# A fused set-attention and maxout kernel: x cast straight into SBUF, transposed on TensorE, four token groups to a score tile, eight PSUM banks in one pool

## The chip, the core and the metric

The kernel runs on one core of one Trainium2 chip. A core has five engines with an instruction queue each: TensorE (PE in the profile, with its weight loads listed apart as PEld), VectorE (DVE), ScalarE (ACT), GpSimd (POOL) and SyncE (SP). Matmul results land in PSUM, which has eight banks of 128 partitions x 512 f32; DVE and ACT move them to SBUF ("eviction"). The metric is the device time of one execution in microseconds (us).

## What is computed

There are B = 4 batches of N = 12544 tokens with C = 128 features, m = 32 inducing points, and a maxout layer with d_ff = 1024.

```python
def mab(q, kv):
    s = scale * (q @ kv.transpose(0, 2, 1))
    s = s - s.max(-1, keepdims=True)
    a = np.exp(s)
    a /= a.sum(-1, keepdims=True) + 1e-09
    return a @ kv
h = mab(I, x)                # (B, 32, C): 32 inducing points look at all tokens
y = mab(x, h)                # (B, N, C): each token looks at the 32 rows of h
g = np.maximum(y @ w1, y @ w2)
out = g @ w_out
```

Both kernels use max(y w1, y w2) = y w1 + relu(y (w2 - w1)), and since y is a weighted mean of the rows of h, both push h through the weights first: hwd = h (w2 - w1) and m1 = h w1 w_out are small. Per token there remain the 32 exponentials E2, relu(E2 hwd) with 1024 values, its product with w_out, E2 m1, and a division by the sum of E2. The maxima are not subtracted.

## The kernel before

**Phase 1** (for each batch, tokens in blocks of 2048, that is 16 groups of 128): GpSimd's queue casts x from f32 to f16, DRAM to DRAM, into `xf16` (`emit_cast`, line 70). SyncE's queue then loads it twice: transposed by a DMA transpose into `xT` (line 113) and plain into `xnat` (line 117). TensorE makes the scores (line 129, 16 matmuls of 32 columns), ACT the exponential `ETg` (line 137), and TensorE accumulates h and its divisor in one PSUM bank over the whole batch (line 152, 16 matmuls of 129 columns a block). `emit_smalls` turns that into hT4, hwdrep (hwd, once for each quarter of the partitions) and m1aug4.

**Phase 2** (tokens in blocks of 512, a "tick"): one matmul gives the scores of 512 tokens with the 32 rows of h repeated four times over the 128 partitions (`emit_s2T`, line 227), and one exponential on ACT evicts them (line 231), so that all four quarters hold the same E2T. `emit_dT_group` (lines 251 to 264) uses the quarters as four row tiles of TensorE: four matmuls of 32 rows for four of the eight 128-wide slices of d_ff. Each fills a bank (tags dT0 to dT3), and the eight results of a tick are evicted with relu, the even ones by DVE (line 264), the odd ones by ACT (line 260). `emit_final_pair_mm` (lines 285 and 293) adds up nine matmuls for each of two token groups; DVE divides (lines 311 and 312), and GpSimd's queue stores 512 tokens at a time (line 323).

PSUM is shared out by tag: four banks for dT, two for the final pairs, one ("psA") for all score tiles, one ("haug") for the accumulation and the small steps. Phase 1 of batch b+1 is spread over the ticks of batch b by `tick_jobs`; the emission order and the pools set the order on each engine.

Of the kernel before, what the change touches and what calls it, by code (L numbers as in the profile page):

```python
# [12 lines left out]
ALU = mybir.AluOpType  # L13

T_BLK = 2048
T_BLK2 = 512
RELU_ON_ACT = (1, 3, 5, 7)
# [3 lines left out]
def kernel(  # L21
# [9 lines left out]
    nc = tc.nc  # L31

# [4 lines left out]
    assert C == 128 and M == 32 and J % 128 == 0  # L37
    scale = 1.0 / math.sqrt(C)

    p1_starts = list(range(0, N, T_BLK))  # L40
    p1_sizes = [min(T_BLK, N - s) for s in p1_starts]
    p2_starts = list(range(0, N, T_BLK2))
    p2_sizes = [min(T_BLK2, N - s) for s in p2_starts]
    NB1 = len(p1_starts)
    NB2 = len(p2_starts)
    for s in p1_sizes + p2_sizes:
        assert s % 128 == 0
    MAXCH1 = T_BLK // 128
    MAXCH2 = T_BLK2 // 128

    consts = ctx.enter_context(tc.tile_pool(name="consts", bufs=1))
    xtp = ctx.enter_context(tc.tile_pool(name="xtp", bufs=1))
    xnp = ctx.enter_context(tc.tile_pool(name="xnp", bufs=1))
    sb2 = ctx.enter_context(tc.tile_pool(name="sb2", bufs=2))
    sb3 = ctx.enter_context(tc.tile_pool(name="sb3", bufs=3))
    relup = ctx.enter_context(tc.tile_pool(name="relup", bufs=3))
    outp = ctx.enter_context(tc.tile_pool(name="outp", bufs=3))
    psum = ctx.enter_context(tc.tile_pool(name="psum", bufs=1, space=bass.MemoryType.PSUM))
    dramp = ctx.enter_context(tc.tile_pool(name="dramp", bufs=1, space=bass.MemoryType.DRAM))

    def psum_tile(name, shape, tag, bufs):
        return psum.tile(shape, F32, name=name, tag=tag, bufs=bufs)

    identity32 = consts.tile([M, M], F32, name="identity32")
    make_identity(nc, identity32)

    xf16 = [dramp.tile([N, C], F16, name=f"xf16_{b}", tag=f"xf16_{b}") for b in range(B)]

    def emit_cast(b, r0, r1):
        nc.gpsimd.dma_start(out=xf16[b][r0:r1], in_=x[b, r0:r1])  # L70

    b0_rows = [0, T_BLK, 2 * T_BLK, 4 * T_BLK, N]
    for i in range(len(b0_rows) - 1):
        emit_cast(0, b0_rows[i], b0_rows[i + 1])

    ind_sb = consts.tile([M, C], F32, name="ind_sb")
    nc.sync.dma_start(ind_sb, inducing)
    indT_ps = psum_tile("indT_ps", [C, M], "psA", 1)
    nc.tensor.transpose(indT_ps, ind_sb, identity32)
    inducingT = consts.tile([C, M], F16, name="inducingT")  # L80
    nc.vector.tensor_copy(out=inducingT, in_=indT_ps)

    w1f = consts.tile([C, NJB, 128], F16, name="w1f")
    nc.gpsimd.dma_start(out=w1f, in_=moe_w1.rearrange("c (jb j) -> c jb j", j=128))
    w2f = consts.tile([C, NJB, 128], F16, name="w2f")
    nc.gpsimd.dma_start(out=w2f, in_=moe_w2.rearrange("c (jb j) -> c jb j", j=128))
    w21f = consts.tile([C, NJB, 128], F16, name="w21f")
    nc.vector.tensor_sub(w21f, w2f, w1f)  # L88
    woutp = consts.tile([128, NJB, C], F16, name="woutp")
    nc.gpsimd.dma_start(  # L90
        out=woutp, in_=moe_w_out.rearrange("(jb j) c -> j jb c", j=128)
    )

    xT_tiles = [xtp.tile([C, N], F16, name=f"xT{i}", tag=f"xT{i}") for i in range(2)]
    NXNAT = 3
    xnat_tiles = [
        xnp.tile([128, MAXCH1, 132], F16, name=f"xnat{i}", tag=f"xnat{i}")
        for i in range(NXNAT)
    ]
    for t in xnat_tiles:  # L100
        nc.gpsimd.memset(t[:, :, 128:129], 1.0)

    st = [dict() for _ in range(B)]
    xnat_ctr = [0]

    def emit_p1_dma(b, ib):
        n0 = p1_starts[ib]
        tb = p1_sizes[ib]
        nch = tb // 128
        xT = xT_tiles[b % 2]  # L110
        if ib == 0:
            st[b]["haug"] = psum_tile(f"haug_b{b}", [128, 132], "haug", 1)
# [306 lines left out]
```

## Time and profile before

| | |
|---|---|
| median of 3 runs | 493.05 us (492.4 to 495.18) |
| span of the profiled execution, first to last instruction | 490.7 us |
| TensorE busy / its weight loads | 396.0 / 281.7 us |
| DVE busy / ACT busy | 349.8 / 279.1 us |
| relu evictions on DVE, 128x512 | 384, 683 ns each |
| relu evictions on ACT, 128x512 | 384, 599 ns each |
| score exponentials of phase 2 on ACT, 128x512 | 96, 600 ns each |
| mean granted TensorE clock | 0.997 |

The profile reports one execution. Its time beside the span is not recorded; the median of the runs is 2.35 us above the span. Busy times of TensorE overlap (a matmul's record runs from its start to its modelled end), so distances between starts say more than the sum. In a timeline row stand start, duration, engine, line, operation, output<-inputs and count; in brackets the engine's idle time before it and what ended it.

### The profile page before, as it was taken

What the parts mean: (1) busy time and instruction counts of PE and PEld (TensorE: products, weight loads), DVE (VectorE), ACT (ScalarE), POOL (GpSimd) and SP (SyncE); (2) the same over time, 40 slices, a digit from 0 to 9 for tenths busy, and PEclk for the clock granted to TensorE, in tenths of its full rate; (3) what the DMA queues carried; (4) which work ended last, traced back from release to release, by engine and by line L of the source; (5) the groups of instructions that cost most, each with busy time, mean ns of one, the idle gap of its engine ahead of it and who ended that gap; (6) DMA issues with size and microseconds to landing.
All of it is one profiled execution on the core that took longest, in us unless ns stands there. A gap on an engine that the chain in (4) does not pass through costs nothing.

```text
span 490.7 us, 12616 instructions
## 1 busy us (share of the span) xinstructions
PE 396.0 (81%) x5289; PEld 281.7 (57%) x5289; DVE 349.8 (71%) x818; ACT 279.1 (57%) x533; POOL 86.2 (18%) x132
## 2 busy tenths in 40 slices
PE   0000005589999999899999998999999989999995
PEld 0000005437777776577777775777777746666664
DVE  0000000059889899889899998989889989999995
ACT  1000001157777776677777666777767667777772
POOL 5110000001112111112111121211122112121212
PEclk9999999999999999999999999999999999999998
DMA  8999999999973468336655561444222212222222
GB/s 172 184 233 208 224 202 229 209 232 216 223 152 97 134 166 156 98 100 162 153 95 153 148 157 55 108 123 117 71 67 66 87 33 87 67 74 78 65 87 76
DMA packets 111769, 65.84 MB, mean 134 GB/s; under 512 B 104640, under 2 KB 104672, under 8 KB 111200
## 3 DMA queue, kind: packets, MB, share of 16 engines
q0 software_dynamic: 9968, 39.33, 30.5%
q1 hardware_dynamic: 101744, 25.71, 27.6%
q8 instruction: 41, 0.67, 0.6%
q14 instruction: 16, 0.13, 0.1%
HBM read 40.12 MB, written 38.54 MB: 160 GB/s over the span
## 4 chain that ended last, share of the span: by engine, by line
issue 75%; POOL 15%; DMA 8%; POOLq 1%
POOL out_dram L323 15%; DMA xf<-in_x_dram 8%; POOLq L323 0%; POOL xf L70 0%; POOLq L414 0%; POOL m1aug_b L218 0%; POOL identity masks.py:199 0%; POOL identity masks.py:197 0%; POOLq masks.py:199 0%; POOLq L218 0%; POOLq L403 0%
## 5 line engine op out<-in xcount | busy, mean ns | idle before, releaser
L264 DVE TENSOR_SCALAR relu_b_n<-dT_b_n_j 128x512 f16<-128x512 f32 (+1 forms) x400 | 257.0, 673 | 28.8 <-PE dT_b_n_j L251 22.3
L260 ACT ACTIVATE relu_b_n<-dT_b_n_j 128x512 f16<-128x512 f32 (+1 forms) x400 | 214.3, 590 | 57.8 <-PE dT_b_n_j L251 57.5
L293 PE MATMUL outp_b_n_p<-woutp,relu_b_n 128*128 128x128 f16 x3136 | 219.2, 219 | 0.0
L293 PEld LDWEIGHTS <-relu_b_n 128*128 128x128 f16 x3136 | 192.4, 98 | 1.1 <-issue 1.1
L323 POOL DMA_DIRECT2D out_dram<-outsb_b_n x100 | 75.0, 750 | 371.1 <-DVE outsb_b_n L312 360.0
L251 PE MATMUL dT_b_n_j<-E2T_b_n,hwdrep_b 32*128 32x512 f16 (+1 forms) x800 | 117.9, 381 | 1.0 <-DVE relu_b_n L264 0.5
L285 PE MATMUL outp_b_n_p<-m1aug_b,E2T_b_n 128*128 128x129 f16 x392 | 88.3, 225 | 0.0
L312 DVE TENSOR_TENSOR outsb_b_n<-outp_b_n_p,rp_b_n_p 128x256 f32<-128x256 f32 x196 | 82.5, 421 | 4.6
L231 ACT ACTIVATE E2T_b_n<-s2T_b_n 128x512 f16<-128x512 f32 (+1 forms) x100 | 59.2, 592 | 42.1 <-PE s2T_b_n L227 40.7
L137 ACT ACTIVATE ET_b_n<-sTg_b_n 128x512 f16<-128x512 f32 (+1 forms) x28 | 15.2, 544 | 102.6 <-PE sTg_b_n L129 102.2
L129 PE MATMUL sTg_b_n<-inducingT,xT 128*128 128x32 f16 x392 | 14.5, 180 | 68.5 <-DMA xT<-xf 68.3
L251 PEld LDWEIGHTS <-hwdrep_b 32*128 32x128 f16 x800 | 33.9, 91 | 57.8 <-issue 39.6
L285 PEld LDWEIGHTS <-E2T_b_n 128*128 128x128 f16 x392 | 37.9, 97 | 44.2 <-issue 40.8
L163 DVE RECIPROCAL hrecip_b<-haug_b 32x1 f32<-32x1 f32 x4 | 0.6, 156 | 76.2 <-PE haug_b L152 76.2
L129 PEld LDWEIGHTS <-xT 128*128 128x128 f16 x392 | 12.7, 98 | 70.0 <-DMA xT<-xf 69.6
L152 PE MATMUL haug_b<-xnat,ET_b_n 128*32 128x129 f16 x392 | 32.3, 243 | 12.7 <-DMA xnat<-xf 12.7
L227 PE MATMUL s2T_b_n<-xT,hT_b 128*128 128x512 f16 (+1 forms) x100 | 38.5, 385 | 0.0
L152 PEld LDWEIGHTS <-ET_b_n 128*32 128x32 f16 x392 | 27.1, 107 | 15.2 <-issue 8.7
L311 DVE RECIPROCAL rp_b_n_p<-outp_b_n_p 128x2 f32<-128x2 f32 x196 | 31.5, 161 | 2.8 <-PE outp_b_n_p L293 2.3
L88 DVE TENSOR_TENSOR w21f<-w2f,w1f 128x1024 f16<-128x1024 f16 x1 | 0.7, 693 | 19.5 <-DMA w2f<-in_moe_w_dram 19.5
L70 POOL DMA_DIRECT2D xf<-in_x_dram x16 | 8.2, 511 | 29.8 <-DMA xf<-in_x_dram 24.8
L227 PEld LDWEIGHTS <-hT_b 128*128 128x128 f16 x100 | 9.9, 99 | 4.5 <-issue 4.5
(29 smaller groups left out, 32.9 us busy)
## 6 DMA issues: line engine op xcount, KB each, us to landing
out_dram<-outsb_b_n POOLq DMA_DIRECT2D x96, 256.0 KB, 2.8
xnat<-xf SPq DMA_DIRECT2D x24, 512.0 KB, 4.8
xf<-in_x_dram POOLq DMA_DIRECT2D x12, 784.0 KB, 28.2
xf<-in_x_dram POOLq DMA_DIRECT2D x1, 1088.0 KB, 16.2
xf<-in_x_dram POOLq DMA_DIRECT2D x2, 512.0 KB, 6.2
xf<-in_x_dram POOLq DMA_DIRECT2D x1, 1024.0 KB, 11.4
out_dram<-outsb_b_n POOLq DMA_DIRECT2D x4, 128.0 KB, 2.2
xT<-xf SPq DMA_TRANSPOSE x28, 5.9
```

Of the source, the lines that this page charges most:

```text
L129: nc.tensor.matmul(out=sTg[:, k * M : (k + 1) * M], lhsT=xT[:, n0 + 128 * k : n0 + 128 * (k + 1)], rhs=inducingT, start=True, stop=True,)
L152: nc.tensor.matmul(out=haug[0:M, 0:129], lhsT=ETg[:, k, :], rhs=xn[:, k, 0:129], start=(gchunk == 0), stop=(last and k == nch - 1),)
L227: nc.tensor.matmul(out=s2T_ps[:, 0:tb], lhsT=hT4, rhs=xT[:, n0 : n0 + tb], start=True, stop=True)
L231: nc.scalar.activation(out=E2T[:, 0:tb], in_=s2T_ps[:, 0:tb], func=AF.Exp, scale=scale)
L251: nc.tensor.matmul(out=dT_ps[:, 0:tb], lhsT=hwdrep[32 * q : 32 * (q + 1), jb // 4, 128 * (jb % 4) : 128 * (jb % 4 + 1)], rhs=E2T[32 * q : ...
L260: nc.scalar.activation(out=relu_sb[:, jb, 0:tb], in_=dT_ps[:, 0:tb], func=AF.Relu)
L264: nc.vector.tensor_scalar(out=relu_sb[:, jb, 0:tb], in0=dT_ps[:, 0:tb], scalar1=0.0, scalar2=None, op0=ALU.max,)
L285: nc.tensor.matmul(out=op_ps[:, kk_i, 0:129], lhsT=E2T[:, tslice], rhs=m1aug4[:, 0:129], start=True, stop=False,)
L293: nc.tensor.matmul(out=op_ps[:, kk_i, 0:128], lhsT=relu_sb[:, jb, tslice], rhs=woutp[:, jb, :], start=False, stop=(jb == NJB - 1),)
L311: nc.vector.reciprocal(out=rp[:, 0:npair, :], in_=op_ps[:, 0:npair, 128:129])
L312: nc.vector.tensor_mul(out_sb[:, 2 * pair : 2 * pair + npair, :], op_ps[:, 0:npair, 0:128], rp[:, 0:npair, :].broadcast_to((128, npair, 128)),
L323: nc.gpsimd.dma_start(out=out[b * N + n0 : b * N + n0 + tb, :].rearrange("(k p) c -> p k c", p=128), in_=out_sb[:, 0:nch, :],)
```

## The change

The kernel is written anew; only the arithmetic stays.

- **Loads.** `load_x` reads 16 groups of f32 from DRAM with a cast into an SBUF tile `xn` (ten tiles). A partition now holds consecutive tokens ("(p k)"), so one partition's piece of a load is 8 KB of f32. The DRAM copy, the DMA transposes and the second load are gone. SyncE's queue loads only the inducing points and the three weight matrices, in f32.
- **Transposes.** `p1_transpose` transposes each group on TensorE against an identity, eight into one bank in f16; DVE evicts one bank of a block, ACT the other.
- **Phase 1.** The accumulation has x as the stationary operand and 32 columns moving, restarts with each block and is added up in SBUF by DVE (`hacc`). The divisor is summed from the exponentials, by GpSimd from batch 1 on (`eacc`), and spread over the partitions by a matmul with ones. m1 comes from one product w1 w_out made once at the start (`w1out`).
- **Phase 2.** Tokens go in blocks of 2048 (n = 16 groups; smaller ones at the ends). `stage` makes the scores of four different sets of 512 tokens with four column tiles of TensorE, one for each quarter of the partitions, and one exponential evicts them. `burst` u makes slice u of d_ff for all four quarters, four row-tiled matmuls into four banks. `final` p handles two groups; since a quarter of E2 now belongs to other tokens, m1 has four variants that are zero outside their quarter. The finals of a block run behind the bursts of the next one, one final for each burst.
- **PSUM and order.** All eight banks are one pool. A list of estimated times (`Model`) picks, while the program is built, the bank that it expects free first, and DVE or ACT for each relu. The order on each engine is the written one (`manual_schedule`).

```diff
-    def emit_cast(b, r0, r1):
-        nc.gpsimd.dma_start(out=xf16[b][r0:r1], in_=x[b, r0:r1])
+    def pick(self, n, ready):
+        return min(
+            ("DVE", "ACT"), key=lambda e: max(self.t[e], ready + self.SEM) + self.cost(e, n)
+        )
...
+    xr = x.rearrange("b (p k) c -> b p k c", p=128)
...
+    def load_x(b, i):
+        k0, n = p1_blocks[i]
+        nc.gpsimd.dma_start(out=xn_of(b, i)[:, 0:n, :], in_=xr[b, :, k0 : k0 + n, :])
...
-        nc.sync.dma_start_transpose(xT[:, n0 : n0 + tb], xf16[b][n0 : n0 + tb, :])
+                for j in range(m):
+                    nc.tensor.transpose(ps[:, j, :], xn[:, g + j, :], identity16)
...
+                eng = "DVE" if (g // 8) % 2 == 0 else "ACT"
...
-                out=haug[0:M, 0:129],
-                lhsT=ETg[:, k, :],
-                rhs=xn[:, k, 0:129],
+                    out=ps[:, 0:M],
+                    lhsT=xn[:, j, :],
+                    rhs=et[:, j, :],
...
+                nc.gpsimd.tensor_add(out=acc, in0=acc, in1=et[:, 0:n, :])
...
+            def stage(self):
+                bi, ps = bank([128, 512])
+                for q in range(4):
+                    c0, t = self.chunks(q)
+                    nc.tensor.matmul(
+                        out=ps[32 * q : 32 * (q + 1), 0 : self.width],
+                        lhsT=st[self.b]["hT4"][:, 32 * q : 32 * (q + 1)],
+                        rhs=xT_tiles[self.b % 2][:, c0 : c0 + t, :],
...
+                        tile_position=(0, 32 * q),
...
+                for jj in range(jpb):
+                    for q in range(4):
+                        bi, ps, qt, j0 = banks[q]
+                        jb = j0 + jj
+                        nc.tensor.matmul(
+                            out=ps[:, jj * w : (jj + 1) * w],
+                            lhsT=st[self.b]["hwd"][32 * q : 32 * (q + 1), 128 * jb : 128 * (jb + 1)],
+                            rhs=self.e2[32 * q : 32 * (q + 1), 0:w],
...
+                for q in range(4):
+                    bi, ps, qt, j0 = banks[q]
+                    eng = model.pick(512, end)
...
+        for i in range(NP1):
+            p1_transpose(0, i)
+            p1_scores(0, i)
+            p1_accum(0, i)
+            if i == NP1 - 2:
+                nc.vector.tensor_sub(w21, w2f, w1f)
+                nc.scalar.copy(out=woutp, in_=woutf)
...
+        for i in range(NP1):
+            load_x(1, i)
+        small_h(0)
+        small_hwd(0)
+        small_m1(0)
...
+            for blk in all_blocks[b]:
+                for u in range(blk.nburst):
+                    blk.burst(u)
+                    if queue:
+                        blk_p, p = queue.pop(0)
+                        blk_p.final(p)
+                    for f, *a in jobs.pop(s, ()):
+                        f(*a)
+                    if u == min(2, blk.nburst - 1) and id(blk) in nxt:
+                        nxt[id(blk)].stage()
+                    s += 1
+                queue += [(blk, p) for p in range(blk.nburst)]
```

The blocks of batch 0 have 2, 4, 8, five times 16, and 4 groups, those of the other batches six times 16, and 2. So there are 30 stages, 196 bursts, 196 finals and 784 relu evictions of 512 elements. `jobs` spreads phase 1 of the next batch over the steps of this one (a "step" is a burst and a final), and in steps 42 to 45 its small products.

On TensorE's queue in the middle of phase 2, before: one score matmul (s2T), four row tiles (dT) that read the same E2T, and the first of nine matmuls of a final pair.

```order
L227 LDWEIGHTS hT_b_4612
L227 MATMUL s2T_b_n_5338<-xT_108,hT_b_4612 128x512
L251 LDWEIGHTS hwdrep_b_4614
L251 MATMUL dT_b_n_j_5344<-E2T_b_n_5169,hwdrep_b_4614 128x512
L251 LDWEIGHTS hwdrep_b_4614
L251 MATMUL dT_b_n_j_5347<-E2T_b_n_5169,hwdrep_b_4614 128x512
L251 LDWEIGHTS hwdrep_b_4614
L251 MATMUL dT_b_n_j_5350<-E2T_b_n_5169,hwdrep_b_4614 128x512
L251 LDWEIGHTS hwdrep_b_4614
L251 MATMUL dT_b_n_j_5353<-E2T_b_n_5169,hwdrep_b_4614 128x512
L285 LDWEIGHTS E2T_b_n_5078
```

The same place now, in batch 1: the last two of the four column tiles of a stage, a burst (e_1_16 is the E2 of the block that begins at group 16), and the first matmul of a final of the block before (e_1_0).

```order
L302 LDWEIGHTS hT_1_2418
L302 MATMUL ps_3156<-xT_93,hT_1_2418 32x512
L342 LDWEIGHTS hwd_2455
L342 MATMUL ps_3163<-e_1_16_2793,hwd_2455 128x512
L342 LDWEIGHTS hwd_2455
L342 MATMUL ps_3164<-e_1_16_2793,hwd_2455 128x512
L342 LDWEIGHTS hwd_2455
L342 MATMUL ps_3165<-e_1_16_2793,hwd_2455 128x512
L342 LDWEIGHTS hwd_2455
L342 MATMUL ps_3166<-e_1_16_2793,hwd_2455 128x512
L375 LDWEIGHTS e_1_0_2638
L375 MATMUL ps_3175<-m_1_127,e_1_0_2638 128x129
```

The score matmul stood in front of every second group of four; the stage stands in front of every eighth. The final now reads a block that is eight steps old.

On ACT's queue in phase 2, before: two relus for each group of four tiles, and an exponential for every four relus.

```order
L231 ACTIVATE E2T_b_n_7217<-s2T_b_n_7215 128x512
L260 ACTIVATE relu_b_n_7069<-dT_b_n_j_7224 128x512
L260 ACTIVATE relu_b_n_7069<-dT_b_n_j_7230 128x512
L260 ACTIVATE relu_b_n_7144<-dT_b_n_j_7262 128x512
L260 ACTIVATE relu_b_n_7144<-dT_b_n_j_7268 128x512
L231 ACTIVATE E2T_b_n_7292<-s2T_b_n_7290 128x512
```

Now, late in batch 2: three relus of each burst of four (ps numbers that follow each other are one burst), and no exponential in this stretch.

```order
L361 ACTIVATE relu_80_6615<-ps_6776 128x512
L361 ACTIVATE relu_80_6615<-ps_6777 128x512
L361 ACTIVATE relu_80_6615<-ps_6778 128x512
L263 CAST hwd_6811<-ps_6815 128x512
L361 ACTIVATE relu_80_6615<-ps_6818 128x512
L361 ACTIVATE relu_80_6615<-ps_6819 128x512
L361 ACTIVATE relu_80_6615<-ps_6821 128x512
```

Over the whole program ACT has 512 of the 784 relus and DVE 272; in the last batch ACT has 23 of the 32 of each block of 16 groups.

On GpSimd's queue at the start, before: casts of batch 0 (xf_0), the weights, and then the casts of all other batches ahead of the first store.

```order
L70 DMA xf_0_86<-in_x_dram 64x8704
L84 DMA w1f<-in_moe_w_dram 128x1024
L86 DMA w2f<-in_moe_w_dram 128x1024
L90 DMA woutp<-in_moe_w_out_dram 128x8x128
L101 MEMSET xnat_110 128x16
L101 MEMSET xnat_111 128x16
L101 MEMSET xnat_112 128x16
L70 DMA xf_1_87<-in_x_dram 32x12544 x4
L218 MEMSET m1aug_b_387 128x1
L70 DMA xf_2_88<-in_x_dram 32x12544 x4
L70 DMA xf_3_89<-in_x_dram 32x12544 x4
```

Now: seven loads for batch 0, then three for batch 1 that find free tiles; the load behind them (again xn_82) waits for phase 1 of batch 0 to have used that tile.

```order
L109 DMA xn_82<-in_x_dram 128x2048
masks.py:197 MEMSET identity_94 128x128
masks.py:199 ISA
masks.py:199 AFFINE_SELECT identity_94<-identity_94 128x128
masks.py:197 MEMSET identity_95 128x128
masks.py:199 AFFINE_SELECT identity_95<-identity_95 128x128
L109 DMA xn_83<-in_x_dram 128x2048
L109 DMA xn_84<-in_x_dram 128x2048
L109 DMA xn_85<-in_x_dram 128x2048
L109 DMA xn_86<-in_x_dram 128x2048
L109 DMA xn_87<-in_x_dram 128x2048
L109 DMA xn_88<-in_x_dram 128x256
```

Only batch 0 stands between the first load and phase 2 now; the rest is loaded beside it.

More of the change, by code (lines that the diff above doesn't have):

```diff
@@ L36 @@
     NJB = J // 128
-    assert C == 128 and M == 32 and J % 128 == 0
+    K = N // 128
+    assert C == 128 and M == 32 and NJB == 8 and N % 128 == 0
     scale = 1.0 / math.sqrt(C)
[L40 to L48, printed above, removed]
@@ L96 @@
[L96 to L112, printed above, removed]
-        nc.sync.dma_start_transpose(xT[:, n0 : n0 + tb], xf16[b][n0 : n0 + tb, :])
-        xn = xnat_tiles[xnat_ctr[0] % NXNAT]
-        xnat_ctr[0] += 1
-        st[b][("xn", ib)] = xn
-        nc.sync.dma_start(
-            out=xn[:, 0:nch, 0:128],
-            in_=xf16[b][n0 : n0 + tb, :].rearrange("(k p) c -> p k c", p=128),
-        )
@@ L392 @@
+        while queue:
+            blk_p, p = queue.pop(0)
+            blk_p.final(p)
 _INS = ['x', 'inducing', 'moe_w1', 'moe_w2', 'moe_w_out']
```

638 lines of the change are left out of this document (359 added, 279 removed).

## The prediction

> **What bounds the kernel now.** I read the slices first, then the timeline of the start, then one tick of the last batch, and last the groups by shape for single durations.
>
> ```profile
> PE 396.0 (81%) x5289; PEld 281.7 (57%) x5289; DVE 349.8 (71%) x818; ACT 279.1 (57%) x533; POOL 86.2 (18%) x132
> PE   0000005589999999899999998999999989999995
> DVE  0000000059889899889899998989889989999995
> DMA  8999999999973468336655561444222212222222
> ```
>
> A slice is 12.3 us. TensorE and DVE do nothing for six slices while the DMA engines are full, then both run at eight or nine tenths. So there are two parts with two limits: a start, and a steady part.
>
> ```profile
> 6.96 0.50 POOL L70 DMA_DIRECT2D xf<-in_x_dram  x1 [0.56 <-DMA xf<-in_x_dram]
> 9.57 0.49 POOL L70 DMA_DIRECT2D xf<-in_x_dram  x1 [2.11 <-DMA xf<-in_x_dram]
> 20.89 51.91 SPq L113 DMA_TRANSPOSE xT<-xf  x1
> 94.27 0.61 PE L129 MATMUL sTg_b_n<-inducingT,xT 128*128 128x32 f16 x16
> 94.98 0.60 ACT L137 ACTIVATE ET_b_n<-sTg_b_n 128x512 f16<-128x512 f32 x1 [4.00 <-PE sTg_b_n L129]
> 95.63 0.10 PEld L152 LDWEIGHTS <-ET_b_n 128*32 128x32 f16 x1 [0.85 <-ACT ET_b_n L137]
> 102.98 0.61 PE L251 MATMUL dT_b_n_j<-E2T_b_n,hwdrep_b 32*128 32x512 f16 x3
> ```
>
> GpSimd's queue waits at 6.96 and 9.57 for the first two casts of 2048 tokens: a block takes 2.61 us. Batch 0 would be there by about 20 us, but the second DMA transpose sits 51.91 us on SyncE's queue behind the casts of the other batches. Phase 2 begins at 102.98, a fifth of the span.
>
> ```profile
> 430.96 0.69 PE L251 MATMUL dT_b_n_j<-E2T_b_n,hwdrep_b 32*128 32x512 f16 x4
> 431.58 0.23 PE L285 MATMUL outp_b_n_p<-m1aug_b,E2T_b_n 128*128 128x129 f16 x1
> 432.60 0.38 PE L227 MATMUL s2T_b_n<-xT,hT_b 128*128 128x512 f16 x1
> 432.91 0.61 PE L251 MATMUL dT_b_n_j<-E2T_b_n,hwdrep_b 32*128 32x512 f16 x4
> 433.46 0.23 PE L285 MATMUL outp_b_n_p<-m1aug_b,E2T_b_n 128*128 128x129 f16 x1
> 434.57 0.69 PE L251 MATMUL dT_b_n_j<-E2T_b_n,hwdrep_b 32*128 32x512 f16 x4
> 254.91 0.39 PE L251 MATMUL dT_b_n_j<-E2T_b_n,hwdrep_b 32*128 32x512 f16 x4
> 255.24 0.23 PE L285 MATMUL outp_b_n_p<-m1aug_b,E2T_b_n 128*128 128x129 f16 x1
> ```
>
> By distances of starts, a tick of 512 tokens (430.96 to 434.57) is 3.61 us: groups of four tiles 0.62 and 0.55, two final pairs of 1.02, a score matmul 0.31, and 0.09 of turning round before the last group. At 254.91 a group finds its four banks free and takes 0.33. So TensorE loses 0.29 and 0.22, **0.51 us in a tick, waiting for banks**. Who holds them:
>
> ```profile
> 429.93 1.28 DVE L264 TENSOR_SCALAR relu_b_n<-dT_b_n_j 128x512 f16<-128x512 f32 x2
> 431.12 0.16 DVE L311 RECIPROCAL rp_b_n_p<-outp_b_n_p 128x2 f32<-128x2 f32 x1
> 431.46 0.69 DVE L264 TENSOR_SCALAR relu_b_n<-dT_b_n_j 128x512 f16<-128x512 f32 x1 [0.17 <-PE dT_b_n_j L251]
> 433.00 0.16 DVE L311 RECIPROCAL rp_b_n_p<-outp_b_n_p 128x2 f32<-128x2 f32 x1
> 433.53 1.28 DVE L264 TENSOR_SCALAR relu_b_n<-dT_b_n_j 128x512 f16<-128x512 f32 x2
> 433.51 1.08 ACT L260 ACTIVATE relu_b_n<-dT_b_n_j 128x512 f16<-128x512 f32 x2
> ```
>
> DVE returns to the same place after 3.60 us and idles 0.17 of it: it is the limit, with four relus at 0.60 (429.93 to 431.12 for two) and two divisions at 0.53 (433.00 to 433.53). ACT needs 1.08 for two relus, of which the second costs 0.48.
>
> **The steady part after.** A step is a burst and a final. TensorE: 0.09 of turning, 0.33 and 1.02 make 1.44 us. Evictions: DVE has 272 of 784 relus, 1.39 for each of 196 steps: 0.53 + 1.39 x 0.60 = 1.36. ACT has 2.61 at 0.48, 1.25, and an eighth of an exponential, 0.06. All are under 1.44, so **TensorE becomes the limit**, with little room. The four banks of a burst are free some 2 us after its start (0.33, 0.3 until the first eviction, three on ACT at 0.48), the next burst comes after 1.44, and with eight banks in one pool it finds four others, one of them perhaps late. For such waits I take 8 us, a sixth of the 0.255 a step that is lost now (196 x 0.255 = 50); the bounds are 0 and 50. 196 steps: 282 us.
>
> *Stages.* 30 of them in place of 100 score matmuls of 0.31. No row shows column tiles: if they run side by side like the row tiles, 0.33; if one after another, four times 0.31, 1.24. I take 0.5, nearer to the row tiles, with a change of tiling: 15 us (10 to 37).
>
> *Phase 1 beside phase 2*, three times, and the start, which is phase 1 alone:
>
> ```profile
> 254.37 0.51 PEld L129 LDWEIGHTS <-xT 128*128 128x128 f16 x16
> 258.18 1.09 PE L152 MATMUL haug_b<-xnat,ET_b_n 128*32 128x129 f16 x16
> 92.28 1.89 PE L152 MATMUL haug_b<-xnat,ET_b_n 128*32 128x129 f16 x16 [1.99 <-DMA xnat<-xf]
> 71.00:105.00 34.00, 19.58 (x216) 14.63 (x217) 2.86 (x6) 6.51 (x12) 0.00 (x0) 1.00 1.16 224
> L169 PE MATMUL hT_ps_b<-identity,h_b 32*128 32x32 f32 x4 | 1.0, 252 | 0.7 <-DVE h_b L165 0.7
> L177 PE MATMUL hwd_ps_b<-w21f,hT_b 128*128 128x512 f16 x8 | 3.5, 436 | 3.6 <-DVE hwdrep_b L185 2.1 <-DVE hT_b L171 1.5
> L200 DVE CAST hw1T_b<-hw1T_ps_b 128x1024 f16<-128x1024 f32 x4 | 4.9, 1215 | 0.0
> L101 POOL MEMSET xnat<- 128x16 f16 x3 | 0.4, 245 | 0.0
> 99.30 0.15 DVE L163 RECIPROCAL hrecip_b<-haug_b 32x1 f32<-32x1 f32 x1 [76.19 <-PE haug_b L152]
> ```
>
> Sixteen scores hold TensorE from 254.37 to 254.91, 0.54; the new accumulation has the same shape (128 x 128 stationary, 32 moving), 0.54 in place of 1.09. Transposes move 128 columns like the final's matmuls, nine in 0.51, so 0.9 for sixteen; they are new work, and bounded by nothing below that row and twice it above. 1.98 for a block, 6.125 blocks: 12.1 a batch, 36.5 for three. DVE gets 1.2 more for each block (row L200, an upper end since its source is f32), 12.8 with 12 relus and 8 divisions, beside TensorE's 13.5 with phase 1 (8 x 1.44 + 1.98): covered, and if that cover went, up to 22 us for the 18 full blocks. ACT gets two queued evictions' worth, 1.08, and an exponential, 0.5: 11.7 with 20 relus, covered. GpSimd's additions have only the memset row to go by, 245 ns for 16 elements; even at 32 times that, 7.8 us, they fit in the six steps (8.6 us) between them. Behind a waiting load on its queue stand the stores; four output tiles of two steps each (11.5 us) cover that. The small products: two of 436 ns, an f32 one and a 128-column one beside them, with a short wait, 1.5 each, 4.5.
>
> *The start.* The first block lands at about 7.5 (6.96 above, a little later since the weights share the engines), the others 2.61 apart. On TensorE each waits for its own evictions, since the order is as written. At 92.28 sixteen matmuls take 1.89, later 1.09: TensorE runs 1.7 times slower while it is 58% busy (19.58 of 34.00 in the row of the stretch 71 to 105), although the granted clock there reads 1.00 (third from the end). With that pace a block costs: transposes 1.6, ACT's 1.08 with 0.1 on each side, 1.36 from the first score to the accumulation (94.27 to 95.63), 0.54: 4.8 us, which is slower than the DMA, so its 2.61 is hidden. Six blocks: 36.3. Then the weights: eight f32 transposes (0.25 each by row L169, 0.61 by the matmul at 102.98; I take 0.44), a copy, eight products: 5.3. The last block of two groups 1.6. From the reciprocal to the first dT was 3.7 (99.30 to 102.98), with an f32 sum ahead, 4.6. **First burst at 48 us** (38 to 58), against 102.98.
>
> A page of the Trainium skill speaks against a fast start here: "TensorE: Matmul & The Clock Gate", Part 1, says that TensorE runs at half rate until it has been busy for a window of about 3.4 us, and Part 4 that transposes don't count as busy. By that rule the start stays slow throughout, as in the sum; without it, at the later pace, a block takes 4.1 and the time is 4 us less. The trace agrees as to the slow pace at 92.28; no row has transposes.
>
> *Ramp and tail.* The first 15 bursts come with 7 finals, so eight have evictions alone to set the pace (four relus by two engines, some 1.1 to 1.3 against the 0.42 counted): 7 us.
>
> ```profile
> 484.79 0.61 PE L293 MATMUL outp_b_n_p<-woutp,relu_b_n 128*128 128x128 f16 x8
> 487.03 0.71 POOL L323 DMA_DIRECT2D out_dram<-outsb_b_n  x1 [0.97 <-DVE outsb_b_n L312]
> ```
>
> From the last matmuls (484.79) to the end (490.7) it is 5.9, of which 0.5 is counted: 5.4 for the last division and store.
>
> **Sum.** 48 + 282 + 15 + 36.5 + 4.5 + 7 + 5.4 + 8 (waits) = 406.4 of span, against 490.7. The median stands 2.35 above the span: **409 us**. Of the 84 us, 55 come from the start; the steady part gives 30 (fewer bank waits and score matmuls, less what the transposes add).
>
> **Rivals.**
> *(1) The bank waits stay.* If TensorE still loses 0.255 in each step, that is 50 in place of 8: **451 us**. For it: ACT's share in the last batch, 23 of 32 relus, is 2.88 x 0.48 + 0.06 = 1.44, just what a step lasts; engine and bank are fixed by estimates while the program is built, so nothing corrects a drift. Against it: eight banks where a group had four, and evictions at 1.36 and 1.31 on average. It decides once either engine needs over 1.44 on average.
> *(2) The start gains less*, since the loads land late: writing 128 partitions could go slower than DRAM to DRAM, or the weights on SyncE's queue starve as the transpose at 20.89 did. At half the rate a block takes 5.2, over the 4.8; weights behind ten loads come at 29, in time at the known rate, at 55 at half of it. First burst then at about 66: **427 us**. Against it: the same bytes are read, and only ten loads can run ahead.
> *(3) Slower than before: TensorE stays at its slow pace in phase 2.* A final at 1.7 times is 1.77; 0.75 more. From 113 slow finals of 196 on the 84 us are gone; all of them and the bursts slow (0.33 x 0.7 = 0.23 more) give 409 + 192 = **601 us**. For it: the pace at 92.28 and idle gaps at every wait. Against it: the gaps forecast are under a microsecond, and at 254.91 to 433.46 the pace is full with waits of 0.3. The clock-gate page of the Trainium skill would have it slow again only after an idle window of about 3.4 us; by that rule this rival needs a long wait again and again.
>
> **How the numbers follow.** The forecast gets 0.74, rival 1 0.14, rival 2 0.07, rival 3 0.03, and 0.02 that it is still better than my low end. Low end: start 9 less, waits 8 less, stages 4 less: 388. High end: start 10 more, waits 10 more, column tiles partly one after another 9 more: 438, which takes in rival 2 and a third of rival 1. About 0.5% is what a measurement of this kernel can tell from no change. Faster by more than that: all but rival 3 and a sliver, 0.965; within 0.5% 0.005; slower 0.03.
>
> **What would show it.** Right: first burst at 38 to 58; steps of 1.44 to 1.5 between the first matmuls of finals in the last batch, a group of four in 0.33 to 0.4; DVE and ACT both idle now and then for TensorE. A stage from final to burst in 0.5. Wrong: steps of 1.7 with TensorE waiting for relus (rival 1); phase 1 of batch 0 waiting for loads (rival 2); nine matmuls in 0.9 late in the trace (rival 3). What would upset the sum most is a price that no row has: column tiles, transposes into f16, and GpSimd's additions.

## The result and the profile after

| | before | after |
|---|---|---|
| median, the same chip | 493.24 us (4 runs) | **390.02 us** (4 runs, 389.41 to 390.45) |
| ratio after / before | | 0.789, 95% interval 0.785 to 0.793 |
| profiled execution: span | 490.7 us | 387.6 us |
| first burst (first dT) | 102.98 us | 45.52 us |
| TensorE / DVE / ACT busy | 396.0 / 349.8 / 279.1 us | 356.9 / 315.7 / 314.6 us |
| DMA packets, bytes moved | 111769, 65.84 MB | 13339, 40.98 MB |

The forecast was 409 us with a range of 388 to 438: on the right side, 19 us too high. The engines' shares and the slices of the page of after, a slice being 9.7 us:

```profile
PE 356.9 (92%) x5769; PEld 282.3 (73%) x5769; DVE 315.7 (81%) x772; ACT 314.6 (81%) x602; POOL 90.7 (23%) x157
PE   1667689999999999999999999999999999999995
DVE  1334369999999898998989888999899888888873
ACT  1344269988888898888999889988999999999970
```

The six empty slices of TensorE have become one that is nearly empty, and a stretch of five follows in which it is about 60 to 80% busy. After that it is at nine tenths until the last slice, while DVE and ACT fall to eight now and then: the bound has moved from DVE to TensorE. The timeline of the start shows what fills the stretch:

```profile
8.34 1.89 PE L148 MATMUL ps<-identity,xn 128*128 128x128 f16 x16 [4.95 <-DMA xn<-in_x_dram]
11.34 0.40 PE L164 MATMUL ps<-inducingT,xT 128*128 128x32 f16 x8 [0.78 <-ACT xT L156]
12.42 0.59 PE L186 MATMUL ps<-et,xn 128*128 128x32 f16 x16 [0.69 <-ACT et L173]
12.84 1.87 PE L148 MATMUL ps<-identity,xn 128*128 128x128 f16 x16
39.68 3.17 PE L233 MATMUL ps<-esum,ones 128*128 128x32 f32 x14
45.52 0.61 PE L342 MATMUL ps<-e,hwd 32*128 32x128 f16 x16 [0.52 <-ACT e L312]
```

Only the first block waits for a load. From then on a block takes 4.48 us (8.34 to 12.84, and then alike): transposes at the slow pace (1.87; in phase 2 sixteen take 1.06, see e9), a wait for ACT's copy, one for the exponential. Next, a stage and steps of the last batch:

```profile
318.66 0.40 PE L302 MATMUL ps<-xT,hT 128*32 128x512 f16 x4
318.99 0.39 PE L342 MATMUL ps<-e,hwd 32*128 32x512 f16 x4
320.43 0.39 PE L342 MATMUL ps<-e,hwd 32*128 32x512 f16 x4
321.87 0.39 PE L342 MATMUL ps<-e,hwd 32*128 32x512 f16 x4
323.31 0.39 PE L342 MATMUL ps<-e,hwd 32*128 32x512 f16 x4
323.42 0.17 DVE L393 RECIPROCAL rp<-ps 128x2 f32<-128x2 f32 x1 [0.22 <-PE ps L383]
319.61 11.15 ACT L361 ACTIVATE relu<-ps 128x512 f16<-128x512 f32 x22
```

Four bursts stand 1.44 apart, none with a bracket: TensorE waits for nobody, and DVE idles 0.22 for it. The stage costs 0.33. ACT is all but full as well: 22 relus without a bracket. Started one by one, its 23 relus and one exponential of such a block of eight steps leave a single gap, 0.29 us in 11.85. So TensorE is the limit here by a hair. Over the whole run the waits of TensorE at the bursts are these (us, times, longest):

```profile
PE ps L342 <- ACT e L312: 6.0, 7, 1.6
```

There is no row in which a burst waits for a relu. By itself that proves little, since a wait inside a group of four shows only in the group's length (e11 below). The length says the same: of some 190 bursts behind 60 us nearly all take 0.39 or 0.40, and behind the ramp sixteen take 0.43 to 0.55, about 1 us in all. **Where the 103 us came from:** 57.5 are the earlier start (102.98 - 45.52). In the last batch 512 tokens took 3.61 us and now take two steps and a quarter of a stage, 2.96; were it so everywhere, 98 such blocks would give 64. The transposes beside phase 2 take back some 17 (18.4 blocks of 0.90, below). That estimate, 47, stands beside the 45.6 left over; that it comes so close is partly luck, since it leaves out the cheaper accumulation and the ramp.

### The profile page after: what moved, and what is told of

It is laid out like the page before. It is cut to its first block, busy times and chain, and to the rows that moved or that the text cites. A ratio compares the mean times of both kernels' runs of the same rounds, so it can differ in the third digit from the quotient of the medians.

```text
span 387.6 us, 13426 instructions
## 1 busy us (share of the span) xinstructions
PE 356.9 (92%) x5769; PEld 282.3 (73%) x5769; DVE 315.7 (81%) x772; ACT 314.6 (81%) x602; POOL 90.7 (23%) x157
## 2 busy tenths in 40 slices
DMA packets 13339, 40.98 MB, mean 106 GB/s; under 512 B 2112, under 2 KB 3680, under 8 KB 13280
## 4 chain that ended last, share of the span: by engine, by line
PE 72%; ACT 14%; issue 7%; POOL 2%; DMA 2%; DVE 1%; POOLq 0%
PE ps L383 34%; PE ps L342 14%; ACT relu L361 10%; PE ps L375 8%; PE ps L148 7%; PE ps L186 3%; PE ps L164 2%; ACT xT L156 2%; POOL out_dram L403 2%; DMA xn<-in_x_dram 2%; PE ps L302 2%; ACT et L173 1%; PE ps L233 1%; ACT e L312 1%; ACT hwd L263 1%
## 5 line engine op out<-in xcount | busy, mean ns | idle before, releaser
L361 ACT ACTIVATE relu<-ps 128x512 f16<-128x512 f32 x512 | 265.9, 627 | 17.5 <-PE ps L342 16.0
L383 PE MATMUL ps<-woutp,relu 128*128 128x128 f16 x3136 | 218.2, 219 | 0.0
L383 PEld LDWEIGHTS <-relu 128*128 128x128 f16 x3136 | 192.9, 98 | 0.1
L357 DVE TENSOR_SCALAR relu<-ps 128x512 f16<-128x512 f32 x272 | 179.0, 683 | 10.3 <-PE ps L342 9.4
L403 POOL DMA_DIRECT2D out_dram<-o x100 | 54.3, 543 | 263.2 <-DVE o L395 180.1
L395 DVE TENSOR_TENSOR o<-ps,rp 128x256 f32<-128x256 f32 x196 | 83.2, 424 | 7.0 <-DVE rp L393 0.3
L375 PE MATMUL ps<-m,e 128*128 128x129 f16 x392 | 88.4, 226 | 0.1
L342 PE MATMUL ps<-e,hwd 32*128 32x512 f16 (+2 forms) x896 | 80.7, 361 | 6.2 <-ACT e L312 6.0
L375 PEld LDWEIGHTS <-e 128*128 128x128 f16 x392 | 38.0, 97 | 42.9 <-issue 42.1
L393 DVE RECIPROCAL rp<-ps 128x2 f32<-128x2 f32 x196 | 32.6, 166 | 20.3 <-PE ps L383 15.1
L164 PEld LDWEIGHTS <-xT 128*128 128x128 f16 x392 | 13.3, 99 | 8.9 <-ACT xT L156 5.1
L173 ACT ACTIVATE et<-ps 128x512 f16<-128x512 f32 (+1 forms) x28 | 15.5, 554 | 4.5 <-PE ps L164 4.5
```

Source lines behind the costliest of these rows:

```text
L164: nc.tensor.matmul(out=ps[:, j * M : (j + 1) * M], lhsT=xT_tiles[b % 2][:, k0 + j, :], rhs=inducingT, start=True, stop=True,)
L342: nc.tensor.matmul(out=ps[:, jj * w : (jj + 1) * w], lhsT=st[self.b]["hwd"][32 * q : 32 * (q + 1), 128 * jb : 128 * (jb + 1)], rhs=self.e2 ...
L357: nc.vector.tensor_scalar(out=dst, in0=src, scalar1=0.0, scalar2=None, op0=ALU.max)
L361: nc.scalar.activation(out=dst, in_=src, func=AF.Relu)
L375: nc.tensor.matmul(out=o, lhsT=self.e2[:, 128 * tt : 128 * (tt + 1)], rhs=st[self.b]["m1"][:, q, 0:129], start=True, stop=False,)
L383: nc.tensor.matmul(out=o[:, 0:128], lhsT=self.relu[:, jb, 128 * kc : 128 * (kc + 1)], rhs=woutp[:, jb, :], start=False, stop=(jb == NJB - 1),)
```

## The experiments

e1 to e4 are one run each, on one chip; the others have 4 runs each. The kernel before took 492.8 to 493.4 us in all of them. After is 390.02.

**e1: before, with the casts of later batches held back.** Was it the casts that held the start up?

```diff
-        if k == 2:
-            for i in range(4):
-                emit_cast(1, ...)
+        if k == NB1 - 1:
+            emit_gated_casts(1, st[0][("ETg", NB1 - 2)][:, 0, 0:1])
...
-            for i in range(4):
-                emit_cast(b + 2, ...)
+            emit_gated_casts(b + 2, st[b]["m1aug4"][:, 0:1])
```

> The kernel before, with the casts of batch 1 held back until phase 1 of batch 0 is nearly over, and those of batches 2 and 3 until the batch two ahead of them enters phase 2. Theory (the start was long because the casts of the other batches held up the DMA transposes of batch 0): the first dT matmul comes at 50 to 65 us in place of 103, and the time falls by 35 to 50 us. Rival (the DMA transposes themselves are slow, and only TensorE's transposes shorten the start): first dT at 90 or later, time within 10 us of before.

481.28 us. The timeline of e1, SyncE's queue (SPq), TensorE and DVE:

```profile
28.75 4.00 SPq L123 DMA_TRANSPOSE xT<-xf  x1
58.38 0.61 PE L261 MATMUL dT_b_n_j<-E2T_b_n,hwdrep_b 32*128 32x512 f16 x3
72.51 21.45 SPq L123 DMA_TRANSPOSE xT<-xf  x1
74.50 0.61 PE L139 MATMUL sTg_b_n<-inducingT,xT 128*128 128x32 f16 x16 [7.74 <-DMA xT<-xf]
97.71 0.61 PE L139 MATMUL sTg_b_n<-inducingT,xT 128*128 128x32 f16 x16 [10.13 <-DMA xT<-xf]
206.14 0.42 DVE L322 TENSOR_TENSOR outsb_b_n<-outp_b_n_p,rp_b_n_p 128x256 f32<-128x256 f32 x1 [11.18 <-DMA out_dram<-outsb_b_n]
```

The first dT comes at 58.38 rather than 102.98, so the casts did hold it up. But the total was missed: 12 us in place of 35 to 50. A DMA transpose holds SyncE's queue for 4.00 us with no cast beside it and for 21.45 beside the casts of batch 2, which were issued from 73.22 on. In phase 2 TensorE stands for 7.74 and for 10.13 us until transposed loads have landed. Later, at 207.22, it stands for 10.38 because DVE waits 11.18 for a store, shortly after the casts of batch 3 were issued. These three waits are 28 of the 33 us that the earlier start did not bring. So the gain is given back where the casts now run; the third wait has to do with stores, not with transposes. The way over DRAM and the DMA transposes is a cost that this order did not take away; no other order was tried.

**e2: the changed kernel with four banks for bursts, two for finals, two for the rest.**

```diff
-    def bank(shape, dtype=F32):
-        i = model.bank()
+    def bank(shape, dtype=F32, among=(6, 7)):
+        i = model.bank(among)
...
-                    bi, ps = bank([128, 512])
+                    bi, ps = bank([128, 512], among=(0, 1, 2, 3))
...
-                bi, ps = bank([128, 512])
+                bi, ps = bank([128, 512], among=(4, 5))
```

> The changed kernel, but bursts keep to four PSUM banks, finals to two, everything else to the last two, as the tags of before had it. Theory (eight banks in one pool took the bank waits away): a bank is held for 0.33 + 0.3 + up to three evictions of 0.48, about 2 us, so a step goes from 1.44 to 1.7 to 2.0, and the time up by 50 to 110 us. Rival (the waits went because ACT has fewer exponentials and more relus): a step stays under 1.5, time up by less than 8 us.

430.41 us, 40 more: less than expected, far over the rival. But the planner had changed more than banks: its times hang on them, and it had moved 102 relus from ACT to DVE (busy 369.6 us, after 315.7).

**e3: the changed kernel with two relus of each burst on each engine.**

```diff
-                    eng = model.pick(512, end)
+                    eng = ("DVE", "ACT")[q % 2]
```

> The changed kernel, but of each burst two relus always go to DVE and two to ACT, as before. Theory (TensorE is the limit only since ACT took relus from DVE): DVE needs 0.53 + 2 x 0.60 = 1.73 for a step, so steps of 1.73 in the last batch and the time up by 40 to 57 us. Rival (with eight banks the split hardly matters): up by less than 8 us.

424.94 us, 35 more, just below the range of the theory. DVE in the timeline of e3:

```profile
344.85 1.28 DVE L357 TENSOR_SCALAR relu<-ps 128x512 f16<-128x512 f32 x2
346.58 1.28 DVE L357 TENSOR_SCALAR relu<-ps 128x512 f16<-128x512 f32 x2
```

DVE returns every 1.73 us with no idle time: two relus and a division are more than TensorE's 1.44. Since e2 had nearly this split, its loss could have been this one and not the banks'.

**e11: the banks of e2, every relu on the engine that it has in the changed kernel.**

```diff
-                    eng = model.pick(512, end)
+                    eng = {"A": "ACT", "D": "DVE"}[PICKS[npick[0]]]
+                    npick[0] += 1
...
```

> Four banks for the bursts, two for the finals, two for the rest, as in e2, but every relu on the engine on which the changed kernel has it (512 on ScalarE, 272 on VectorE); in e2 the planner, whose times hang on the banks, had moved 102 of them to VectorE. Theory: e2 lost its 40 us by VectorE, as e3 did, and not by the banks; with the old split the kernel takes 390 to 396. Rival: the bursts must wait for their four banks to be emptied, and the kernel takes 410 or more.

431.49 us (ratio to before 0.874, 0.869 to 0.878). My theory fell: it is the banks. TensorE and ACT in the timeline of e11:

```profile
340.34 0.64 PE L355 MATMUL ps<-e,hwd 32*128 32x512 f16 x4
340.76 3.26 ACT L375 ACTIVATE relu<-ps 128x512 f16<-128x512 f32 x6 [0.21 <-PE ps L355]
342.02 0.74 PE L355 MATMUL ps<-e,hwd 32*128 32x512 f16 x4
343.80 0.64 PE L355 MATMUL ps<-e,hwd 32*128 32x512 f16 x4
```

A burst now lasts 0.64 to 0.74, since its last matmul waits for the bank that ACT empties last: in the burst at 340.34 three start at once and the fourth at 340.60, when ACT's third relu, begun at 339.94, is over. ACT, after six relus, idles 0.21 in turn until the first matmuls of the next burst are done. A step is 1.73 (340.34 to 343.80 are two). With the 3:1 split ACT closes the loop, with the nearly even one of e2 DVE does; only with other banks to hand does the split of 512 to 272 bring 1.44. The edit also holds the finals and everything else to two banks each; the waits that the trace shows in these steps are those of the bursts. Each of the two alone takes back 35 to 41 us: the pool and the split work together, so their shares don't add up.

**e4: every stage made four times**, matmuls and exponential.

```diff
+                for rep in range(4):
...
```

> The changed kernel with each stage (score matmuls and exponential) made four times over, three of them only repeated, so that the score work per token is that of before. Theory (four groups to a score tile are worth their TensorE time, 0.33 for each stage, since TensorE is the limit): 90 more stages, up by 30 us, and up to 45 if ACT (1.44 more in eight steps) becomes the limit. Rival (score work was hidden): up by less than 8 us.

427.92 us, 38 more, 1.26 for each of 30 stages. TensorE in the timeline of e4:

```profile
329.17 1.05 PE L303 MATMUL ps<-xT,hT 128*32 128x512 f16 x16
332.16 0.40 PE L342 MATMUL ps<-e,hwd 32*128 32x512 f16 x4 [1.94 <-ACT e L312]
333.37 1.06 PE L383 MATMUL ps<-woutp,relu 128*128 128x128 f16 x8
336.98 0.61 PE L383 MATMUL ps<-woutp,relu 128*128 128x128 f16 x8
```

The stage is on the path. Sixteen column-tiled matmuls of 512 columns take 1.05, so they run side by side; that is 0.65 more a stage by distance of starts (338.02 to 339.00 in place of 0.33). The rest is waiting for ACT's four exponentials (15.5 us of such rows in all, 6.0 in the changed kernel; 1.94 at each of the three turns of batches) and a thing I had not expected: after the gap shown here eight products take 1.06 in place of 0.61, for some 4 us. Behind the same gap at 143.40 some are slow too, behind that at 238.58 none.

**e9: phase 1 of the last batch left out.** This kernel computes batch 3 with the h of batch 2 and the transposed tokens of batch 1, so its output is not that of the others. The edit:

```diff
+            if nb == 3:
+                st[3].update(st[2])
...
-                    if nb + 1 < B:
+                    if nb + 1 < 3:
```

> The changed kernel without phase 1 of the last batch: neither its loads nor its transposes, scores and sums are made, and batch 3 is computed with the h of batch 2 on the transposed tokens of batch 1. Theory: TensorE sets the pace where phase 1 of one batch runs beside phase 2 of another, so what is left out falls off the time in full: 6.1 blocks of 1.67 us, some 1.5 us of small products and the wait of 0.7 at the turn of the batches, 11 to 13 in all, 377 to 379. Rival: there VectorE and ScalarE are the bound (they have the copies and the sums besides the relus), and TensorE's part is hidden: less than 5 or more than 18 us.

376.73 us (ratio to before 0.763, 0.759 to 0.767), 13.3 less, just over the theory's 11 to 13. Phase 1 is paid for in TensorE's time; one block in the timeline of the changed kernel, and then the last batch's first burst there:

```profile
156.20 1.06 PE L148 MATMUL ps<-identity,xn 128*128 128x128 f16 x16
157.19 0.39 PE L342 MATMUL ps<-e,hwd 32*128 32x512 f16 x4
158.54 0.55 PE L164 MATMUL ps<-inducingT,xT 128*128 128x32 f16 x16
159.02 0.39 PE L342 MATMUL ps<-e,hwd 32*128 32x512 f16 x4
161.81 0.56 PE L186 MATMUL ps<-et,xn 128*128 128x32 f16 x16
162.29 0.40 PE L342 MATMUL ps<-e,hwd 32*128 32x512 f16 x4
302.49 0.40 PE L342 MATMUL ps<-e,hwd 32*128 32x512 f16 x4 [0.70 <-ACT e L312]
```

By distances 0.99, 0.48 and 0.48, each in place of a turn of 0.09: 1.68 a block, 10.3 a batch. The timeline of e9:

```profile
39.90 1.73 PE L233 MATMUL ps<-esum,ones 128*128 128x32 f32 x14
216.08 0.40 PE L342 MATMUL ps<-e,hwd 32*128 32x512 f16 x4 [0.70 <-ACT e L312]
289.68 0.40 PE L342 MATMUL ps<-e,hwd 32*128 32x512 f16 x4 [0.81 <-ACT e L312]
```

From its first burst to that of the last batch, batch 2 takes 73.60 here (216.08 to 289.68) and 85.18 in the changed kernel (217.31 to 302.49). So 11.6 are phase 1: the 10.3 and 1.3 for the small products. The wait at the turn of the batches stays, against the theory. Most of the rest lies in the start, where nothing was changed: the f32 product takes 1.73 and not 3.17, and the first burst comes 1.2 earlier. The 3.17 is the odd one: in e2, e3, e4 and e11 this product takes 1.73 as well.

**e5: transposes one block ahead in batch 0.** The start, now 45 us, is what is left to gain.

```diff
+        p1_transpose(0, 0)
         for i in range(NP1):
-            p1_transpose(0, i)
+            if i + 1 < NP1:
+                p1_transpose(0, i + 1)
             p1_scores(0, i)
-            p1_accum(0, i)
+            if i > 0:
+                p1_accum(0, i - 1)
+            if i == NP1 - 1:
+                p1_accum(0, i)
```

> The changed kernel with phase 1 of batch 0 written in another order for TensorE: the 16 transposes of the next block ahead of the scores of this one, the accumulation of the block before behind them. Nothing is added or left out. Theory: in the start a block costs 4.48 us because TensorE waits in turn for the copy, the scores' copy and the exp (transposes 1.87, then about 1 for the ACT copy, 0.6 for the exp); with other work in these waits a block costs TensorE's own time at the slow pace, 1.87 + 0.8 + 0.6 = 3.3, so the first burst comes 6 to 8 us earlier (38 to 40) and the kernel takes 382 to 385. Rival: the period of 4.48 is that of the loads, and the first burst stays within 2 us of 45.5. Second rival: the denser work also takes TensorE to its fast pace (16 transposes in about 1.0 instead of 1.87), then the period is 2.5 to 2.9, that of the loads, and the gain is 10 or more.

380.81 us (ratio to before 0.771, 0.768 to 0.775): 9.2 less than after. TensorE in the timeline of e5:

```profile
17.07 1.58 PE L148 MATMUL ps<-identity,xn 128*128 128x128 f16 x16
19.86 1.07 PE L148 MATMUL ps<-identity,xn 128*128 128x128 f16 x16 [0.42 <-DMA xn<-in_x_dram]
23.41 1.07 PE L148 MATMUL ps<-identity,xn 128*128 128x128 f16 x16 [1.69 <-DMA xn<-in_x_dram]
35.64 0.61 PE L342 MATMUL ps<-e,hwd 32*128 32x128 f16 x16 [0.52 <-ACT e L312]
```

The second rival came nearest. From about 18 us the transposes run at the fast pace, the period is then 2.8 to 3.6, and TensorE waits for loads. The first burst comes 9.9 earlier.

**e6: matmuls that nobody reads in the waits of the start**, the order left as it was.

```diff
+        fill(14)
         for i in range(NP1):
             p1_transpose(0, i)
+            fill(4)
             p1_scores(0, i)
+            fill(3)
```

> The changed kernel with matmuls whose result nobody reads (128x512 on a tile of zeros): 14 ahead of the first transposes, 4 behind the transposes and 3 behind the scores of each block of batch 0. Theory: TensorE's pace in the start hangs on how densely it has been working; kept busy it turns 16 chunks in about 1.0 us instead of 1.87, the block period falls from 4.48 to 3.2 to 3.6, the small f32 products shorten too, and the first burst comes 7 to 12 us earlier. Rival: the slow pace in the start is another thing (the loads beside it, the chip's clock), then each 128x512 takes about 0.43 us, the 7 of a block cost 3 us of which half lies in waits, and the first burst comes 5 to 10 us later.

385.00 us (0.780, 0.776 to 0.784), 5.0 less than after. TensorE in the timeline of e6 (dz is the tile of zeros):

```profile
3.68 5.11 PE L142 MATMUL ps<-dz 128*128 128x512 f16 x14 [0.28 <-DVE inducingT L440]
8.85 1.06 PE L155 MATMUL ps<-identity,xn 128*128 128x128 f16 x16
12.50 1.05 PE L155 MATMUL ps<-identity,xn 128*128 128x128 f16 x16
38.95 0.61 PE L349 MATMUL ps<-e,hwd 32*128 32x128 f16 x16 [0.63 <-ACT e L319]
```

Sixteen transposes take 1.05 instead of 1.89 from the first on: the slow pace of the start is TensorE's own, and it ends with work, useful or not. The block period is 3.65 and the first burst comes 6.6 earlier, both just short of the theory. At the first burst the pace is slow again (0.61 for what takes 0.40 in e10), after waits of 0.78 and 0.63.

**e7: the seven sums of batch 0 folded before the f32 product.**

```diff
+        small_fold0()
         small_h(0)
```

> The changed kernel with the seven partial sums of batch 0 added up by one VectorE reduction (128x32 from 128x224) before the f32 product with the ones, which then is one product and not seven. Theory: the 3.17 us row of that product falls to about 0.45 and the reduction costs 0.5, so the first burst comes 2.0 to 2.5 us earlier and the time falls by as much (387 to 388.5). Rival: the product was waiting for the last reduction of the block anyway, and the time falls by less than 1.

389.76 us (0.789, 0.785 to 0.792): no difference that can be told. DVE and TensorE in the timeline of e7:

```profile
40.64 0.53 DVE L230 TENSOR_REDUCE esum_f<-esum 128x32 f32<-128x224 f32 x1
41.31 0.61 PE L242 MATMUL ps<-esum_f,ones 128*128 128x32 f32 x2 [1.06 <-DVE esum_f L230]
```

TensorE now waits 1.06 for the fold. The first burst is 0.9 earlier than in the profile of after, not 2.0; but the 3.17 us that the theory started from is that one execution's (e9), and where the unfolded product takes 1.73 the first burst comes at 44.29 to 45.02 without any fold, against 44.59 here.

**e8: e5, e6 (with 2 fills a block) and e7 together.**

> The changed kernel with all three edits of the start: transposes one block ahead, unread matmuls (14 ahead of the first transposes, 2 a block), and the folded sum. Theory: with TensorE at its fast pace the block period is that of the loads, 2.5 to 2.9, so the first burst comes at 30 to 34 instead of 45.5, and the first steps after it, which ran slow, gain 1 to 3 more: 373 to 379. Rival: the gain at the start is given back at the ramp or at the load of batch 1, and the time stays above 382.

380.51 us (0.770, 0.767 to 0.774), as e5 alone, between the theory and its rival: the fast pace from the start is worth nothing once the loads set the period (first burst 35.62).

**e10: e8 without the fold, and fills in the ramp too**, behind the last sums and the first stages.

```diff
                         nxt[id(blk)].stage()
+                        if blk is flat[0]:
+                            fill(6)
+                        elif blk is flat[1]:
+                            fill(4)
...
+        fill(3)
         small_h(0)
+        fill(2)
         small_hwd(0)
```

> The changed kernel with the transposes one block ahead (as in e5) and unread matmuls in the waits between the last sums of phase 1 and the third block of phase 2 (3, 2, 2, 6 and 4 of them, each 128x512), nothing in the start itself. Theory: the steps of the ramp run at the slow pace (8 products 1.06 us instead of 0.61, 16 transposes 1.81 instead of 1.06) because TensorE stood still for 1 to 1.6 us before them; with these waits filled they run at the fast pace and the kernel gains 2 to 4 us over e5's 380.8. Rival: the ramp's pace is set by the waits for the exp, and the time stays within 1 us of e5 or rises.

**377.81 us** (0.765, 0.762 to 0.768), the best of all, 3.0 under e5, as the theory has it, and 12.2 under after. Against what its expectation says, it also had the fills of e8 in the start. TensorE in the timeline of e10:

```profile
38.64 0.40 PE L349 MATMUL ps<-e,hwd 32*128 32x128 f16 x16 [0.24 <-ACT e L319]
39.04 0.61 PE L390 MATMUL ps<-woutp,relu 128*128 128x128 f16 x8
```

The second burst waits 0.24 for its exponential (1.57 in e5), and the products behind it take 0.61 and not 1.06.

**e12: e10 without the fills of the start.**

> e5 with the unread matmuls of the ramp alone (3, 2, 2, 6 and 4). The kernel of e10_ramp also had those of e8 in the start (14 ahead of the first transposes and 2 a block), which its expectation left out. Theory: in the start the loads set the period and TensorE comes to its fast pace by itself once the transposes run a block ahead, so the fills of the start are worth nothing and the time stays within 1 us of e10's 377.81. Rival: without them TensorE comes to the ramp at the slow pace, and the time is that of e5 again, 379.5 to 382.

380.33 us (378.09 to 380.83; ratio 0.769, 0.764 to 0.774): the rival, by three of the four runs; the fourth, 378.09, is as fast as e10. TensorE in the timeline of e12, an execution of 380.83:

```profile
29.30 1.09 PE L471 MATMUL ps<-woutp,w1T 128*128 128x128 f16 x8 [1.83 <-ACT w1T L467]
32.31 3.20 PE L240 MATMUL ps<-esum,ones 128*128 128x32 f32 x14
35.32 1.04 PE L142 MATMUL ps<-dz 128*128 128x512 f16 x2
38.88 0.62 PE L349 MATMUL ps<-e,hwd 32*128 32x128 f16 x16
```

Behind a wait of 1.83 us after the weights' transposes TensorE is at the slow pace (the f32 product takes 3.20, in e10 1.75), and the fills, slow themselves (two take 1.04, in e10 0.60), delay the first burst: 38.88 instead of e10's 36.42. The last six fills bring the fast pace back by 41 us. So here fills paid only where no gap before them had already slowed TensorE.

## Why the prediction came out as it did

Direction and mechanism were right; single terms were off, all but the steps too high, so the errors added up. The largest are phase 1 beside phase 2 (6 us), the stages (5) and the waits with the ramp (5). Span predicted 406.4, measured 387.6:

- **First burst**: 48, measured 45.52. Errors of both signs are in it. The first block landed later (8.34 for 7.5). A block is 4.48 (4.8 predicted): transposes and copy as taken (2.98 for 2.88), but only the second half of the scores stands behind the copy, so that from there to the accumulation it is 1.08 for 1.36, and the accumulation is 0.42 for 0.54. The weights were dearer in the sum (5.3) than on the chip, some 3 us (35.24 to 38.27); the way from the last block to the first burst was dearer on the chip, 5.9 in place of 4.6, by the 3.17 us sum, which other executions did in 1.73 (e9). Loads hidden: right (e5: at 2.8 to 3.6 us a block they no longer are).
- **196 steps of 1.44**: exact where TensorE is free of phase 1. TensorE became the limit, as said, with ACT just behind it in the last batch.
- **Stages**: 0.5 taken, 0.33 measured: 10 in place of 15. The row-tile end of the bounds held; no further turn of tiling showed.
- **Phase 1 beside phase 2 with the small products**: 41 for three batches; e9 measures 11.6 for one, 35 for three if the others are alike. The transposes cost 0.99 in place of a turn of 0.09, so 0.90, as predicted from the final's matmuls; scores and sums cost 0.39 each in the same way, and 0.54 was taken; the small products 1.3 for 1.5. One slip: VectorE's work for eight steps with a block adds up to 12.6, not 12.8, and the blocks follow each other after six steps. By the prediction's own terms that is 9.4 for DVE and ACT against TensorE's 10.6, still covered.
- **Bank waits and ramp**: 15 taken together, 10 left once the other terms are taken off (387.6 - 45.5 - 282 - 10 - 35 - 4.7). The 8 for bank waits was mis-sized: behind the ramp the bursts that last longer add up to about 1 us. Three turns of batches cost 0.70 each, which no term had, and the ramp is left with the 7 that it was given. Rival 1 had the price right for other kernels: e2, e3 and e11 show that without the pool, or with an even split, 35 to 41 of its 42 us come back. What spoke for it held too: ACT has 0.29 to spare in eight steps.
- **Tail**: 5.4, measured 4.7.
- **Rival 3** (slow pace in phase 2) shows at the ramp, where eight products take 1.06 until some 52 us. Keeping TensorE busy there is worth 2.7 (e8 to e10). In the steady part the longest wait at a burst is 0.70, and the products behind it take 0.61.

The prediction took the slow pace of the start from the row at 92.28 and named a rule of the Trainium skill beside it ("TensorE: Matmul & The Clock Gate", Parts 1 and 4). As to after, the trace agrees: the transposes at 50.38 still take 1.91. That transposes run or keep TensorE slow is not borne out: e6 has sixteen in 1.05, and in e5 they make up most of the work after which the pace rises. The idle window of about 3.4 us in Part 1 is longer than the gaps behind which TensorE was slow here, 1.83 (e12) and 1.94 (e4).

What stays open: what share of idle time, over what stretch, brings the slow pace back; how much of the 57 us of the start is due to the casts' DRAM copy and how much to the DMA transposes (e1 moved both), and what sets the 2.8 to 3.6 us in which loads follow each other in e5.

## What to carry to other kernels

When a kernel overlaps matmuls with evictions in step, count banks and evictors as one loop: a set of banks that is refilled only after its own eviction costs 0.3 us a step here, with either split that was tried (e2, e11), and a spare set hides it. An edit that a planner answers with another split has to be repeated with the split held fixed before its loss is put down to the edit. And where TensorE waits again and again, as in this start twice in each 4.48, for 0.6 to 0.8 us, put the next block's matmuls into the waits (e5, 9.2 us), or failing these matmuls that nobody reads (e6, 5.0 us): beside the wait, the pace is to be gained.

## What was not expected of the hardware

- TensorE's pace changes by a factor of 1.7 to 1.8 with its own work (16 transposes 1.89 or 1.05, 8 products 1.06 or 0.61), and the granted clock of the page shows little of it: its mean is 1.000 in after, slow start included, and 0.974 in e5, which is faster.
- The slow pace came behind gaps of 1.83 (e12) and 1.94 us (e4), and lasted for some 4 to 10 us. The length of one gap does not decide it: in e4 the same 1.94 left no slow products at 238.58, in e6 the pace was slow after waits of 0.78 and 0.63 close together, and a single wait of 0.70 at the turn of a batch brought none.
- The pace of one and the same start differs from execution to execution: the f32 product in the start took 3.17 us in after and 1.73 in e2, e3, e4, e9 and e11.
- A DMA transpose holds SyncE's queue for 4.00 us alone and for 13.54 and 21.45 beside casts from DRAM to DRAM (e1).
- Copying a transposed bank of f16 (128x1024) costs DVE 0.69 us; ACT needs 1.01 for it.
